# Another written order for a fused attention and two-layer kernel: new places for its steps, twelve element sums on another engine, longer early fillers, input buffers named by group

## The chip, the cores and the metric

The kernel runs on one core of one Trainium2 chip. The metric is the device time of one launch in microseconds (us). Before the change three runs took 276.94, 276.41 and 276.31 us; the median, 276.41 us, is the time before. The profile is of one further execution, told of below.

Five engines with a queue each work side by side: PE (TensorE, the matrix products), DVE (VectorE), ACT (ScalarE), POOL (GpSimd) and SP (SyncE, here a queue that only issues DMAs). Each takes its own instructions strictly in the order in which the program emits them; between engines only semaphores order the work.

## The reference

```
scores = (q_c @ k_c.T) / sqrt(64)          # per batch and head, chunks of 64 rows
scores = scores - max(scores)
attn   = exp(scores); attn = attn / (sum(attn) + 1e-9)
x      = attn @ v_c                        # 4608 tokens x 512
h      = x @ w_in                          # 512 -> 2048
g      = max(0.01 * h, h)
out    = g @ w_out                         # 2048 -> 512, float32
```

q, k and v are float32 of shape (8, 8, 576, 64): 8 batches, 8 heads, 576 rows. Attention is only inside chunks of 64 rows.

## The kernel before

**Groups.** The 4608 tokens are 36 groups of 128 tokens (`u` = 0 to 35). POOL issues the DMAs that bring q and k of a group from HBM and cast them to fp16 (`load_q`, `load_k`, line 93; steps `arrive`), those of v (`load_v`, `load_v_rows`) and the weights. For groups 0 to 9 PE turns q and k (`stage_tq`, `stage_tk`, steps `pe_t`); from group 10 on SP issues DMA transposes (`stage_t`, steps `t`), POOL copies the turned q into its zero-padded place (`stage_q2`, steps `p`, line 446). Then for each group: scores on PE (`s`, line 453), row maximum, subtraction (`m`, `b` on DVE), exponential (`x` on ACT), sum, addition of 1e-9 and reciprocal (`z` on DVE: three instructions, lines 479, 481 and 483), division (`n`, line 489, on DVE or POOL), a second turning (`e` on PE, or `d`: a DMA transpose that SP issues), the product with v (`v` on PE, line 519) and the copy into the ring `xT` (`a` on ACT, line 532).

**Blocks.** The two layers work on blocks of tokens: four of 128 and eight of 512 (`BLOCKS`). Blocks 0 to 5 do the first layer plainly (`mm1`, line 187), blocks 0 to 3 the second as well (`mm2`, line 212). All else uses a fast scheme that makes seven products out of eight: in the first layer steps `f j h i m` (block, half, slice, product m = 1 to 7; line 325), in the second layer steps `m2 j.m.p` (block, product, half; line 373). It needs sums of its operands: of the weights once (`wf`, `vf`), of x for each block (`xf j.h.0` to `.3`, lines 281 and 285) and of g for each block (`sf j.0` to `.3`, in `g_form`): `sf 0` = a21 + a22, `sf 1` = `sf 0` - a11, `sf 2` = a11 - a21 in place (line 350), `sf 3` = a12 - `sf 1` in place (line 352). An `sf` has 128 x 2048 elements of fp16. `sf 0` feeds product 5, `sf 1` product 6, `sf 2` product 7 and `sf 3` product 3. ACT and DVE take the products out of PSUM: copies (`d`, `u2`, `u3`), sums (`+u2`, `+u3`, `+d`, line 237) and the leaky function (`gu2`, `gu3`, `g11`, `g21`, line 198). Two 512-token halves of g (`gT`) and three output buffers (`osb`) turn over; SP issues the saves.

**Order.** A planner has searched an order beforehand; the kernel holds the result. The planning code builds a list of 1403 steps; `ORDER` lists them by number, with the PSUM bank for each step that opens one, and `run()` emits them one by one. What is emitted for one engine therefore keeps the order of that list, and nothing else of the plan (no due time, no duration) reaches the chip. `ON` says for some steps which engine does them. Some entries of `ORDER` hold a filler: `idle()` (line 538) emits useless matmuls on PE ahead of the step, in units of 128 columns, four units to a matmul.

## Time and profile before

| what | us |
|---|---|
| runs: median (lowest, highest) | 276.41 (276.31, 276.94) |
| profiled execution, first to last instruction (its span) | 275.7 |
| what lies around the span, taken as median less span | 0.7 |
| DVE busy | 209.4 |
| ACT busy | 196.3 |
| weight loads busy, beside the matmuls | 230.8 |

How to read it: the span runs from the first to the last instruction of the profiled execution. The profile gives no time of its own for what lies around the span; the 0.7 us is the difference to the median of the runs. A busy PE counts from the start of a matmul to a modelled end, so that two matmuls in a row overlap in the records; the step from start to start is the finer measure.

### The profile page before, as it was taken

To read this page: it belongs to the slowest core of one execution; us is meant where nothing else is said; L and a number is where in the kernel's file an instruction comes from. 1 tells how busy PE (TensorE), PEld (TensorE's weight loads), DVE (VectorE), ACT (ScalarE), POOL (GpSimd) and SP (SyncE) were. 2 spreads that over 40 slices of the span, in tenths; PEclk is the share of its full clock that TensorE was granted. 3 is DMA by queue.
4 is the path that set the end of the run, shared out by engine and by line. 5 is a ranking of instruction groups with operands and counts; after the bars stand their busy time and mean duration, and the time that the engine had idled before them with its cause. 6 is when DMAs were issued, how large, how long until landed. Compare 5 with 4: busy or idle time off the path is not lost.

```text
span 275.7 us, 7655 instructions
## 1 busy us (share of the span) xinstructions
PE 263.9 (96%) x3099; PEld 230.8 (84%) x3099; DVE 209.4 (76%) x376; ACT 196.3 (71%) x370; POOL 158.2 (57%) x199
## 2 busy tenths in 40 slices
PE   4899999999999999999799999999999999999994
PEld 2459678788898899999799999999999989888884
DVE  5786276878889898799778997889998873825462
ACT  6478964767844834899698558899787897467821
POOL 8989685595999991928927888626752020000000
PEclk9999999999999999999999999999999999999999
DMA  9999999999999999999999999969972051040016
GB/s 133 158 190 179 179 167 175 134 157 168 172 160 148 173 173 183 132 138 223 129 131 198 138 173 199 153 148 131 212 154 40 0 137 58 0 155 0 30 49 231
DMA packets 163635, 38.64 MB, mean 140 GB/s; under 512 B 154640, under 2 KB 159248, under 8 KB 163600
## 3 DMA queue, kind: packets, MB, share of 16 engines
q0 software_dynamic: 114384, 18.09, 101.9%
q1 hardware_dynamic: 48176, 19.80, 40.1%
q8 instruction: 24, 0.39, 0.6%
q10 hardware_dynamic: 1040, 0.26, 0.4%
q14 instruction: 11, 0.09, 0.1%
HBM read 36.70 MB, written 9.44 MB: 167 GB/s over the span
## 4 chain that ended last, share of the span: by engine, by line
PE 87%; DMA 5%; ACT 5%; POOL 1%; issue 1%; POOLq 0%
PE oA L373 20%; PE hA L325 14%; PE hT L187 13%; PE oC L373 10%; PE hC L325 7%; PE oB L373 5%; PE oP L212 5%; PE hB L325 4%; PE Sp L453 3%; DMA KT<-k_in 3%; PE xp L519 3%; DMA k_in<-in_k_dram 2%; PE idle L538 1%; ACT VB L118 1%; ACT xT L532 1%; ACT gT L198 1%
## 5 line engine op out<-in xcount | busy, mean ns | idle before, releaser
L373 PEld LDWEIGHTS <-gT 128*128 128x128 f16 x640 | 61.3, 98 | 6.7
L489 POOL TENSOR_TENSOR en<-ex,zi 128x512 f16<-128x512 f16 x23 | 26.5, 1153 | 48.4 <-DVE zi L483 17.3
L237 DVE TENSOR_TENSOR tmp<-hC,tmp 128x512 f32<-128x512 f32 x48 | 32.1, 683 | 20.0 <-PE hC L325 18.3
L187 PE MATMUL hT<-xT,w_inT 128*128 128x128 f16 (+1 forms) x512 | 46.0, 246 | 1.0 <-ACT xT L532 0.9
L187 PEld LDWEIGHTS <-w_inT 128*128 128x128 f16 x512 | 39.4, 98 | 4.7 <-issue 1.3
L325 PEld LDWEIGHTS <-VF 128*128 128x128 f16 x512 | 39.4, 98 | 2.7
L93 POOL DMA_DIRECT2D q_in<-in_q_dram x39 | 33.6, 866 | 5.2 <-DMA w_outT<-in_moe_w_out_dram 2.1
L93 POOL DMA_DIRECT2D k_in<-in_k_dram x39 | 33.6, 865 | 2.3 <-DMA k_in<-in_k_dram 1.2
L446 POOL COPY QZ<-QT 64x512 f16<-64x512 f16 x52 | 33.2, 639 | 2.7 <-DMA QT<-q_in 0.5
L201 ACT ACTIVATE tmp<-hA 128x512 f32<-128x512 f32 x48 | 27.7, 598 | 8.6 <-PE hA L325 8.0
L198 ACT ACTIVATE gT<-hT 128x512 f16<-128x512 f32 x48 | 26.7, 601 | 8.6 <-PE hT L187 8.6
L373 PE MATMUL oA<-WF,gT 128*128 128x256 f16 x256 | 32.5, 273 | 0.0
L325 PEld LDWEIGHTS <-w_inT 128*128 128x128 f16 x384 | 30.2, 98 | 2.3
L463 DVE TENSOR_REDUCE mx<-Sp 128x8 f32<-128x512 f32 x36 | 24.5, 682 | 8.6 <-PE Sp L453 8.5
L198 ACT ACTIVATE gT<-tmp 128x512 f16<-128x512 f32 x48 | 29.6, 629 | 1.2 <-DVE tmp L237 1.2
L473 ACT ACTIVATE ex<-sh 128x512 f16<-128x512 f32 x36 | 22.7, 629 | 10.3 <-DVE sh L467 10.1
L479 DVE TENSOR_REDUCE z<-ex 128x8 f32<-128x512 f16 x36 | 24.3, 676 | 6.2 <-ACT ex L473 6.1
L325 PE MATMUL hA<-XF,VF 128*128 128x128 f16 (+1 forms) x256 | 27.5, 246 | 0.0
L532 ACT ACTIVATE xT<-xp 128x512 f16<-128x512 f32 x36 | 21.2, 599 | 8.7 <-PE xp L519 8.6
L373 PEld LDWEIGHTS <-S 128*128 128x128 f16 x256 | 24.5, 98 | 2.7
L467 DVE TENSOR_TENSOR sh<-Sp,mx 128x512 f32<-128x512 f32 x36 | 24.4, 683 | 0.5
L201 ACT ACTIVATE hB<-hA 128x512 f32<-128x512 f32 x24 | 13.9, 586 | 12.2 <-PE hA L325 12.1
(77 smaller groups left out, 490.3 us busy)
## 6 DMA issues: line engine op xcount, KB each, us to landing
out_dram<-osb SPq DMA_DIRECT2D x14, 512.0 KB, 4.3
VB<-in_v_dram POOLq DMA_DIRECT2D x14, 288.0 KB, 7.8
q_in<-in_q_dram POOLq DMA_DIRECT2D x31, 128.0 KB, 7.4
k_in<-in_k_dram POOLq DMA_DIRECT2D x31, 128.0 KB, 7.2
w_inT<-in_moe_w_in_dram POOLq DMA_DIRECT2D x8, 256.0 KB, 7.6
w_outT<-in_moe_w_out_dram POOLq DMA_DIRECT2D x4, 512.0 KB, 9.4
out_dram<-osb SPq DMA_DIRECT2D x6, 256.0 KB, 4.9
v_t<-in_v_dram POOLq DMA_DIRECT2D x4, 128.0 KB, 7.6
```

Source lines behind the costliest of these rows:

```text
L93: nc.gpsimd.dma_start(out=t[a - u * G:z - u * G], in_=src[b, :, r:r + z - a, :].rearrange("h p d -> p h d"))
L187: nc.tensor.matmul(out=hT[:, i, :], lhsT=w_inT[:, t, fc * 128:(fc + 1) * 128], rhs=xT[:, t, r0 % RING:r0 % RING + tb], start=(i == 0 and t ...
L198: nc.scalar.activation(out=to, in_=of, func=AFT.Prelu, bias=0.0, scale=1.0, alpha=0.01)
L201: nc.scalar.activation(out=to, in_=of, func=AFT.Copy, bias=0.0, scale=1.0)
L237: (nc.vector if e == "dve" else nc.gpsimd).tensor_tensor(out=to, in0=a, in1=b, op=ALU.add)
L325: nc.tensor.matmul(out=PA[key][:, c, :], lhsT=w[:, t, fc * 128:(fc + 1) * 128], rhs=x[:, t, :], start=(m in (1, 5) and c == 0 and t == 0), ...
L373: nc.tensor.matmul(out=to, lhsT=lhs[:, fc, p * 128:(p + 1) * 128], rhs=rhs[:, fc, :], start=(fresh and fc == 0), stop=(fc == HB - 1), skip ...
L446: nc.gpsimd.tensor_copy(out=QZ[u % NQZ][part, :, :, s, :], in_=QT[u][part].rearrange("p i (e t) -> p i e t", e=2))
L463: nc.vector.tensor_reduce(out=MX[u], in_=SP[u], axis=AXL.X, op=ALU.max)
L467: nc.vector.tensor_tensor(out=SH[u], in0=SP.pop(u), in1=MX.pop(u).unsqueeze(2).to_broadcast((128, 8, CH)), op=ALU.subtract)
L479: nc.vector.tensor_reduce(out=z, in_=E[u], axis=AXL.X, op=ALU.add)
L489: eng.tensor_tensor(out=E[u], in0=ex, in1=ZI.pop(u).unsqueeze(2).to_broadcast((128, 8, CH)), op=ALU.mult)
```

## The change

The code that plans and emits keeps its steps and their numbers; the lists `ORDER` and `ON` are new.

Engines. Of all steps, fourteen are given to another engine. DVE to POOL: `sf 8.2`, `sf 8.3`, `sf 9.3`, `sf 10.2`, `sf 10.3`, `sf 11.3`, and `xf 6.0.3`, `xf 9.0.3`, `xf 10.0.0`, `xf 11.0.3`. POOL to DVE: the divisions `n` of the groups 30, 31, 33 and 34. To allow it, `g_form` and `x_form` take the engine as an argument:

```diff
-        if i == 0:
-            plus(SF[j, 0], a21, a22)
+        if i == 0:
+            plus(SF[j, 0], a21, a22, e)
...
-            (nc.gpsimd if j >= POOL_S else nc.vector).tensor_tensor(out=a21, in0=a11, in1=a21, op=ALU.subtract)
-        else:
-            (nc.gpsimd if j >= POOL_S else nc.vector).tensor_tensor(out=a12, in0=a12, in1=SF[j, 1], op=ALU.subtract)
+            minus(a21, a11, a21, e)
+        else:
+            minus(a12, a12, SF[j, 1], e)
```

(`POOL_S` and `POOL_X` were 20, more than any block, so these sums all ran on DVE before.)

Order. On each engine most steps stand a few places elsewhere: 358 of PE's 447 steps (2.7 places on average, 23 at most), 274 of ACT's 368, 214 of DVE's. The stretch around the second-layer sums of block 8 and the end, by engine, read from `ORDER`:

```
block 8, DVE before : +u2 8.0.3, xf 9.0.0, b 30, xf 9.0.2, xf 9.0.1, sf 8.0, xf 9.0.3, sf 8.1, z 30, sf 8.2
block 8, DVE after  : m 30, xf 9.0.1, +u2 8.0.3, b 30, xf 9.0.2, sf 8.0, m 31, b 31, sf 8.1, +u2 of 7, +u3 9.0.0, +u3 9.0.1,
                      z 30, z 31, n 30, +u2 9.0.1, m 32, +u2 9.0.0, n 31
block 8, POOL after : n 29, xf 9.0.3, arrive 35 (q), sf 8.2, p 33.1, arrive 35 (k), v_in 7, p 33.0, sf 8.3
end, PE before      : f 11.0.3.4, f 11.0.3.3, m2 10.4.0, 11.1.1, 10.4.1, 11.2.0, 11.2.1, 11.5.0, 11.5.1, 11.6.0, 11.6.1,
                      11.7.0, 11.7.1, 11.4.0, 11.3.0, 11.3.1, 11.4.1
end, PE after       : f 11.0.2.3, f 11.0.3.4, m2 11.1.1, 10.4.0, 10.3.0, 11.2.0, 10.3.1, 11.2.1, 11.5.0, 11.6.0, 11.6.1,
                      11.7.0, 11.5.1, 11.7.1, 10.4.1, 11.3.0, 11.4.0, 11.3.1, 11.4.1
end, ACT after      : d 11.0, d 11.1, gu2 11.0.2, gu2 11.0.3, u2 11.0, ...
end, DVE before     : +u2 11.0.3, +u2 of 10, sf 11.0, sf 11.1, sf 11.2, sf 11.3
end, DVE after      : +u2 11.0.2, +u2 11.0.3, sf 11.0, sf 11.1, +u2 of 10, sf 11.2
end, POOL after     : sf 9.3, xf 11.0.3, sf 10.2, sf 10.3, sf 11.3 (before: POOL has nothing there)
```

On SP the transposes keep nearly their order; `t 22` (k) goes from behind the save of block 5 to ahead of the last save of block 4. On POOL `make_identity` goes from the sixth to the first place, and the early loads are in another order: before q1, k1, k2, w_in (2 parts), identity, q2, q3, three of v, k3; after identity, q1, k1, k2, one part of w_in, q2, one part of w_in, q3, k3, one part of w_in, three of v.

Fillers. Before there are seven, of 21, 3, 47, 13, 9, 9 and 6 units (108); after nine, of 39, 28, 12, 14, 32, 5, 25, 30 and 11 units (196), all ahead of or at the first `mm1`. The nine stand close together: nearly every step of PE up to there has one ahead of it.

Buffers. Tiles that took the next free buffer of a tag now take one by the number of their group:

```diff
-    def k_tile():
-        return sbp.tile([128, H, D], FP16, name="k_in", tag="k_in", bufs=NIN)
+    def in_tile(what, u):
+        return sbp.tile([128, H, D], FP16, name=what, tag=f"{what}{u % NIN}", bufs=1)
...
-    def osb_tile():
-        return sbp.tile([128, 2, d_model], FP32, name="osb", tag="osb", bufs=3)
+    def osb_tile(n):
+        return sbp.tile([128, 2, d_model], FP32, name="osb", tag=f"osb{n % 3}", bufs=1)
```

and so for `gT`, `KT`, `QT`, `et`, `en`, `ex`, `sh`, `mx`, `z`. The q buffers were four of two groups each and are eight of one group each. Code for loading q in pairs, which nothing called, is gone. The new dependences in the planning lists (`after`) change nothing that is emitted.

## The prediction

> **What bounds the kernel now.** First the page: busy shares and slices. Then the waits of PE, then PE's own places of waiting in the timeline.

> ```profile
> PE 263.9 (96%) x3099; PEld 230.8 (84%) x3099; DVE 209.4 (76%) x376; ACT 196.3 (71%) x370; POOL 158.2 (57%) x199
> PE   4899999999999999999799999999999999999994
> POOL 8989685595999991928927888626752020000000
> ...
> PE kp L411 <- POOL ident masks.py:199: 2.1, 1, 2.1
> PE Sp L453 <- DMA KT<-k_in: 1.7, 1, 1.7
> PE idle L538 <- DVE zeros L157: 1.5, 1, 1.5
> PE kp L411 <- DMA k_in<-in_k_dram: 1.1, 1, 1.1
> PE hT L187 <- ACT xT L532: 0.9, 2, 0.7
> PE Sp L453 <- ACT QZ L118: 0.4, 1, 0.4
> ```

> PE bounds it: busy 96%, all slices full but the first two, one in the middle and the last. The required matmuls are the same after the change, so only three things can move the end: when PE's steady work starts, how long it waits inside, how long the tail is. Inside there are two kinds of waits to win: 1.7 us for a turned k (group 22, at 134.7 us) and 0.9 us, in two places, for xT.

> ```profile
> 152.62 3.49 PE oA L373 x32
> ...
> 255.02 1.04 PE L373 MATMUL oC<-w_outT,gT 128*128 128x256 f16 x8
> ```

> In the chain 32 matmuls of 256 columns take 3.49 us: 0.109 each, 0.87 for an `m2` step of eight, 0.44 for an `f` step of four. The timeline's record of eight lasts 1.04, 0.17 more: ends are modelled, so each wait is about 0.17 longer than its row says.

> **The change part by part.** *Waits that go.* `s 22` stands two `m2` steps (1.74 us of PE work) later in the new order and the transpose of k 22 two places earlier in SP's queue; that covers 1.7 + 0.17. After `v 9` and `v 11`, PE now has 0.87 and 0.6 us more to do before the first `mm1` of the two halves of block 5, which covers 0.9 in two places. Three waits: 1.7 + 0.9 + 3 x 0.17 = **-3.1 us**. If the landing of other transposes takes their place, up to all of this comes back.

> *The front.* PE's first `mm1` starts at 19.98.

> ```profile
> 7.60 0.53 PE L538 MATMUL idle<-XF 128*128 128x384 f16 x1
> 9.92 0.61 PE L411 MATMUL kp<-ident,k_in 128*128 128x128 f16 x4 [1.05 <-DMA k_in<-in_k_dram]
> ...
> 10.76 4.16 PE L538 MATMUL idle<-XF 128*128 128x512 f16 x12
> ...
> 15.64 0.87 PE L538 MATMUL idle<-XF 128*128 128x512 f16 x4
> 16.87 0.41 PE L453 MATMUL Sp<-KT,QZ 128*128 128x64 f16 x8 [0.36 <-ACT QZ L118]
> 17.11 0.65 PE L538 MATMUL idle<-XF 128*128 128x512 f16 x3
> ...
> 18.04 0.65 PE L538 MATMUL idle<-XF 128*128 128x512 f16 x3
> ...
> 19.20 0.49 PE L538 MATMUL idle<-XF 128*128 128x512 f16 x2
> ...
> 19.98 2.17 PE L187 MATMUL hT<-xT,w_inT 128*128 128x128 f16 x32
> ...
> 16.84 2.44 ACT L118 ACTIVATE VB<-v_t 64x256 f16<-64x256 f16 x6
> ```

> The new first filler (39 units) fits where PE runs 2.4 us of filler and waits 2.1. The other fillers now take 0.53 + 4.16 + 0.87 + 0.65 + 0.65 + 0.49 = 7.35 us for 87 units; nine late units take 0.65 less 0.17, 0.054 each. The 157 new ones are 8.5 us at that, +1.1, against waits of 1.05 and 0.36 that they fill: -0.3. On the other side `a 0`, which the first `mm1` needs, stands behind six VB copies on ACT (16.84 to 19.28), and the v loads now come behind a k load and a part of w_in more. POOL's queue is past the identity (about 0.6 us) one after the other; a k load issues in 0.87, so v comes 1 to 2 us later, while ACT, held up until 15.62 by the late turning of q, is free earlier. I take **0**, between -0.7 and +0.8.

> *Sums on POOL.* DVE had time for them under PE's work; the question is what a long POOL instruction does to DVE. The form groups and three places of the timeline:

> ```profile
> L350 DVE TENSOR_TENSOR gT<-gT 128x2048 f16<-128x2048 f16 x8 | 9.6, 1206 | 0.0
> L446 POOL COPY QZ<-QT 64x512 f16<-64x512 f16 x52 | 33.2, 639 | 2.7 <-DMA QT<-q_in 0.5
> L489 POOL TENSOR_TENSOR en<-ex,zi 128x512 f16<-128x512 f16 x23 | 26.5, 1153 | 48.4 <-DVE zi L483 17.3
> ...
> 87.54 1.04 POOL L489 TENSOR_TENSOR en<-ex,zi 128x512 f16<-128x512 f16 x1
> 87.76 0.84 DVE L481 TENSOR_SCALAR ze<-z 128x8 f32<-128x8 f32 x1
> ...
> 116.63 1.06 POOL L489 TENSOR_TENSOR en<-ex,zi 128x512 f16<-128x512 f16 x1
> 116.84 1.01 DVE L285 TENSOR_TENSOR XF<-xT 128x256 f16<-128x256 f16 x1
> ...
> 190.45 0.17 DVE L481 TENSOR_SCALAR ze<-z 128x8 f32<-128x8 f32 x1
> 190.65 0.20 DVE L483 RECIPROCAL zi<-ze 128x8 f32<-128x8 f32 x1
> 190.77 1.18 DVE L350 TENSOR_TENSOR gT<-gT 128x2048 f16<-128x2048 f16 x1
> 191.09 1.75 POOL L489 TENSOR_TENSOR en<-ex,zi 128x512 f16<-128x512 f16 x1 [2.51 <-DVE zi L483]
> ```

> `ze` lasts 0.17, but 0.84 when a division runs on POOL, and ends with it. The x sum lasts 1.01 and ends 0.16 after POOL's division. The other way round, the division takes 1.75 instead of 1.04 when DVE's sum was there first. So of a POOL instruction and a DVE instruction with two SBUF inputs (or `ze`), the second waits for the whole of the first. Before, POOL's longest was 1.04 for 512 elements. An `sf` has 2048: 4 x 1.04 = 4.16 us, taken; not under 4 x 0.64 = 2.6 (the copy with one input), not over 4.6 (the mean of 1.153).

> [...]

> *Block 8.* Let E be the end of `f 8.0.3.3`, the last product that `sf 8.0` needs. DVE does `+u2`, `b 30`, `xf 9.0.2` (0.68, 0.68, 0.41; ACT's leaky step lies beside), so `sf 8.0` runs from about E+2.6 to E+3.8. POOL has had time for `xf 9.0.3` and one DMA issue and starts `sf 8.2` at E+4.0 (it starts 0.24 after its releaser at 191.09). DVE does `m 31` and `b 31`, which read PSUM, and wants `sf 8.1` at E+5.2: it waits until E+8.0 and ends at E+9.2. PE between E and `m2 8.6.0`: two `m2`, twelve `f`, three small steps, 1.74 + 5.2 + 0.7 = 7.7. PE waits 9.3 - 7.7, about **+1.5** (0 with 2.6 us on POOL; 2.0 with 4.6). DVE is then some 2.9 us behind, and POOL, behind two copies and two issues, takes `sf 8.3` about when DVE wants `ze 31` and `n 30`. Those would wait up to 4 us; then `d 30`, `d 31`, and `v 30`, `v 31` on PE are late by 0 to 3 us: **+0.7**, the lower half, as four more us of PE work lie ahead of them.

> *The end.*

> ```profile
> 259.47 1.67 ACT L198 ACTIVATE gT<-tmp 128x512 f16<-128x512 f32 x3
> ...
> 261.17 1.23 DVE L237 TENSOR_TENSOR S<-gT 128x2048 f16<-128x2048 f16 x1 [0.73 <-ACT gT L198]
> ...
> 262.44 1.23 DVE L234 TENSOR_TENSOR S<-S,gT 128x2048 f16<-128x2048 f16 x1
> ...
> 263.58 1.22 DVE L350 TENSOR_TENSOR gT<-gT 128x2048 f16<-128x2048 f16 x1
> 264.71 1.22 DVE L352 TENSOR_TENSOR gT<-gT,S 128x2048 f16<-128x2048 f16 x1
> ...
> 267.95 0.38 ACT L201 ACTIVATE tmp<-oA 128x256 f32<-128x256 f32 x1
> ```

> Now the four sums run in a row on DVE ahead of their products. After: let F be the end of `f 11.0.2.3`. `m2 11.1.1` ends at F+1.31, ACT's `d 11.1` (0.38) at F+1.85, two leaky steps (0.56) at F+3.0; `sf 11.0`, `sf 11.1` end at F+5.5; `+u2` of block 10 ends at F+6.2, and only then comes `sf 11.2`. POOL's `sf 11.3` needs `sf 11.1` and `m2 11.2.1`, which ends at F+0.44+6 x 0.87 = F+5.7: it starts at F+6.0, ahead of `sf 11.2` by 0.2, and holds it until F+10.0; `sf 11.2` ends at F+11.2. PE reaches `m2 11.7.0` three steps after `m2 11.2.1`, at F+8.3. It waits **+3.0** (1.4 at 2.6 us, 3.4 at 4.6; 0.1 if DVE is first, since `sf 11.3` then ends when `m2 11.3.0`, four steps further, comes due). The tail behind the last matmul keeps its steps.

> *The rest.* `sf 9.3` behind `n 35` has about 4.3 us until `m2 9.3.0`, `xf 11.0.3` may come between `sf 10.0` and `sf 10.1`: +0.3 (0 to 1.4). The divisions on DVE cost 0.7 where PE does not wait. Buffers by number: 0, the same distance of reuse; `osb` of block 11 waits for the save of 10.0, some 2 us ahead of need.

> **Sum** against the profiled execution: 275.7 - 3.1 + 0 + 1.5 + 0.7 + 3.0 + 0.3 = 278.1 us of span; with the 0.7 between span and median, **278.8 us**.

> **The rivals.**
> *The sums are hidden* (the other side): DVE is first at both places, or POOL's sum is near 2.6 us, and only the waits go: 275.7 - 3.1 + 0.3 + 0.7 = 273.6. For it: at the end the lead is 0.2 us, in which each of ACT's and POOL's starts counts; the slice row has POOL empty there. It decides from `sf 11.2` starting before F+6.0. Against it: three rows of full waiting, and in block 8 a lead of 1.2 us.
> *One lock only*: the end alone, 275.7 - 3.1 + 3.0 + 0.3 + 0.7 = 276.6; block 8 alone, 275.8.
> *Block 8 runs away*: `ze 31` and `n 30` wait the whole 4 us, +3 instead of +0.7, or a wait for another turned tile stays: 281.

> **How the numbers follow.** Forecast 0.43, hidden 0.27, one lock 0.20, runaway 0.10. About 0.2%, 0.55 us, is what a measurement can tell from no change: same is 275.86 to 276.96. Faster: the hidden case and a fifth of the one-lock case, 0.31. Same: the rest of it, 0.16. Slower: 0.53. The forecast's own range is 277.3 to 280.3 (POOL's sum at 2.6 or 4.6 us). The whole range reaches to the centre of the hidden case and to the runaway: 273.4 to 281.0. Both signs hold much of it.

> **What would show it.** POOL rows of 128x2048 near 4.2 us; a DVE sum `sf 8.1` and `sf 11.2` of 4 to 5 us instead of 1.2, with PE's `oA` (L373) waiting for DVE 1.5 and 3.0 us. No wait of `Sp` for KT near 135, none of `hT` for xT in block 5. First `mm1` between 19.3 and 20.8. I am wrong if the DVE sums keep 1.2 us beside POOL's.

## The result and the profile after

The changed kernel takes 301.47 us (median of four runs, 298.93 to 302.83) where the kernel before took 276.36 in the same session: 1.0906 of it, interval 1.0843 to 1.0970, so 25 us slower. The forecast was 278.8 with 281.0 as its upper end: slower, but by a tenth of this. Ratios leave disturbed executions out (one of `old_lists` took 1554.57 us, the profiled one of `new_order_short` 347.74), so where a median with its range and a ratio differ below, the ratio is the number to read.

The page of the changed kernel, busy shares and slices:

```profile
PE 274.3 (92%) x3120; PEld 233.5 (78%) x3120; DVE 225.6 (76%) x370; ACT 196.0 (66%) x370; POOL 186.7 (63%) x205
...
PE   7999999999999999998899999858999999499964
...
POOL 9989765767978997494798691997060241550310
PEclk9999999999999999999999999997999999889978
```

The slices of PE that were full now have three holes, at slices 26 to 28, 35 and 39 (7.5 us each: some 187 to 209, 254 to 261 and 284 to 291 us), and in or behind each of them the granted clock of PE (PEclk, the share of full speed that PE is allowed) drops, to 0.50 for 3.41 us each time, which it never did before (1.00 in every stretch of that execution). The waits of PE name the holes (us in total, times, longest):

```profile
PE oA L355 <- DVE S L216: 4.1, 1, 4.1
PE hA L307 <- DVE osb L219: 3.5, 1, 3.5
PE oA L355 <- DVE gT L216: 2.7, 1, 2.7
PE xp L491 <- DMA et<-en: 1.7, 2, 1.0
PE hA L307 <- ACT hB L183: 1.5, 1, 1.5
...
PE Sp L425 <- POOL QZ L418: 1.2, 2, 1.0
PE hA L307 <- DVE XF L216: 0.7, 1, 0.7
```

The lines are those of the changed kernel. Line 216 is `minus`, the subtraction of an `sf` or `xf`; line 219 is `plus`, here the sum that writes an output buffer. Of the rest, 307 is a first-layer and 355 a second-layer product, 425 the scores, 491 the product with v, 461 the division, 453 `ze` (the addition of 1e-9), 418 the copy of a turned q, 183 a copy on ACT. The timeline of the changed kernel at these places, DVE, POOL and PE together (start, duration, engine):

```profile
191.28 2.67 DVE L216 TENSOR_TENSOR XF<-xT 128x512 f16<-128x512 f16 x1
191.50 1.06 POOL L461 TENSOR_TENSOR en<-ex,zi 128x512 f16<-128x512 f16 x1
192.51 1.15 POOL L216 TENSOR_TENSOR XF<-xT,XF 128x512 f16<-128x512 f16 x1
...
195.18 4.05 POOL L216 TENSOR_TENSOR gT<-gT 128x2048 f16<-128x2048 f16 x1 [0.64 <-DVE S L219]
196.33 3.98 DVE L216 TENSOR_TENSOR S<-S,gT 128x2048 f16<-128x2048 f16 x1
200.24 0.68 DVE L219 TENSOR_TENSOR osb<-oC,tmp 128x512 f32<-128x512 f32 x1
200.97 0.60 PE L307 MATMUL hA<-xT,w_inT 128*128 128x256 f16 x4 [3.47 <-DVE osb L219]
203.43 4.05 POOL L216 TENSOR_TENSOR gT<-gT,S 128x2048 f16<-128x2048 f16 x1
203.73 3.78 DVE L453 TENSOR_SCALAR ze<-z 128x8 f32<-128x8 f32 x1
209.73 0.60 PE L307 MATMUL hA<-XF,VF 128*128 128x256 f16 x4 [1.48 <-ACT hB L183]
...
253.48 4.05 POOL L216 TENSOR_TENSOR gT<-gT 128x2048 f16<-128x2048 f16 x1 [1.16 <-DVE S L219]
253.50 5.11 DVE L216 TENSOR_TENSOR S<-S,gT 128x2048 f16<-128x2048 f16 x1
258.67 2.86 PE L355 MATMUL oA<-WF,S 128*128 128x256 f16 x16 [4.09 <-DVE S L216]
...
280.73 4.05 POOL L216 TENSOR_TENSOR gT<-gT,S 128x2048 f16<-128x2048 f16 x1 [13.45 <-PE oB L355]
280.89 4.97 DVE L216 TENSOR_TENSOR gT<-gT 128x2048 f16<-128x2048 f16 x1
285.92 1.11 PE L355 MATMUL oA<-WF,gT 128*128 128x256 f16 x8 [2.71 <-DVE gT L216]
```

Read it in pairs. A POOL sum lasts 4.05 us, and a DVE sum of 1.2 us or a `ze` of 0.17 us that starts behind it ends only after it: `sf 8.1` takes 3.98, `ze 31` 3.78, `sf 10.1` 5.11, `sf 11.2` 4.97. Behind each pair PE waits. At 191.28 a DVE sum of 0.41 lasts 2.67, over two POOL instructions in a row: the division, whose record starts 0.22 behind its own, and the POOL sum behind that. `sf 8.1`, `sf 11.2` and this sum wait for no semaphore in the trace. So here, other than said ahead of the prediction, semaphores are not all that orders the work of two engines. This holding of one engine by another is called the lock below.

Where the 22.9 us between the two profiled executions (spans of 298.6 and 275.7) lie can be added up from the single matmuls: the distance from start to start less the step's own (0.109 for 256 columns and so on), summed by stretch from the first `mm1` on. What the lowered clock costs is inside these sums. The medians are 25.1 apart, because these two executions are not the median ones: the changed kernel's took 300.56, and the one of before was some 1.1 us longer than its median. The 0.7 us set down ahead of the prediction as lying around the span is too small by as much; executions of the kernel before with both numbers on record have 1.7 to 1.9 (276.41 with a span of 274.6).

| stretch, us | before | after | difference | forecast |
|---|---|---|---|---|
| first `mm1` | 19.98 | 20.19 | +0.2 | 0 |
| lost from there to 190 | 4.04 | 7.97 | +3.9 | -3.1 |
| 190 to 220 (blocks 8, 9) | 0.05 | 7.90 | +7.9 | +2.2 |
| 220 to 262 (block 10) | 0.07 | 5.95 | +5.9 | +0.3 |
| 262 to the last matmul | 0.01 | 4.62 | +4.6 | +3.0 |
| behind the last matmul | 3.65 | 4.01 | +0.4 | 0 |
| sum | | | +22.9 | +2.4 |

### The profile page after: what moved, and what is told of

It is laid out like the page before. It is cut to its first block, busy times and chain, and to the rows that moved or that the text cites. A ratio compares the mean times of both kernels' runs of the same rounds, so it can differ in the third digit from the quotient of the medians.

```text
span 298.6 us, 7701 instructions
## 1 busy us (share of the span) xinstructions
PE 274.3 (92%) x3120; PEld 233.5 (78%) x3120; DVE 225.6 (76%) x370; ACT 196.0 (66%) x370; POOL 186.7 (63%) x205
## 4 chain that ended last, share of the span: by engine, by line
PE 52%; DVE 23%; DMA 9%; POOL 7%; ACT 4%; issue 3%; SPq 1%; POOLq 0%; DVEq 0%; ACTq 0%
PE oA L355 13%; PE hA L307 8%; PE hT L169 7%; PE oC L355 6%; PE oP L194 4%; PE hC L307 4%; DVE S L216 3%; DMA w_inT<-in_moe_w_in_dram 3%; DMA QT<-q_in 3%; PE oB L355 3%; DVE gT L216 3%; DMA k_in<-in_k_dram 2%; DVE z L451 2%; DVE ze L453 2%; PE hB L307 2%
## 5 line engine op out<-in xcount | busy, mean ns | idle before, releaser
L355 PEld LDWEIGHTS <-gT 128*128 128x128 f16 x640 | 61.8, 99 | 10.5 <-DVE gT L216 3.0
L418 POOL COPY QZ<-QT 64x512 f16<-64x512 f16 x52 | 40.2, 776 | 23.8 <-DMA QT<-q_in 22.3
L219 DVE TENSOR_TENSOR tmp<-hC,tmp 128x512 f32<-128x512 f32 x48 | 31.9, 682 | 18.2 <-ACT tmp L183 11.6
L461 POOL TENSOR_TENSOR en<-ex,zi 128x512 f16<-128x512 f16 x19 | 19.9, 1050 | 33.6 <-DVE zi L455 32.6
L355 PE MATMUL oA<-WF,gT 128*128 128x256 f16 x256 | 33.4, 277 | 2.7 <-DVE gT L216 2.7
L180 ACT ACTIVATE gT<-hT 128x512 f16<-128x512 f32 x48 | 26.8, 597 | 11.4 <-PE hT L169 11.2
L355 PEld LDWEIGHTS <-S 128*128 128x128 f16 x256 | 25.4, 102 | 8.4 <-DVE S L216 4.4
L307 PE MATMUL hA<-XF,VF 128*128 128x128 f16 (+1 forms) x256 | 28.1, 247 | 2.2 <-ACT hB L183 1.5
L216 POOL TENSOR_TENSOR gT<-gT,S 128x2048 f16<-128x2048 f16 x4 | 16.2, 4060 | 19.1 <-PE oB L355 19.1
```

The source lines that it names most:

```text
L180: nc.scalar.activation(out=to, in_=of, func=AFT.Prelu, bias=0.0, scale=1.0, alpha=0.01)
L216: (nc.vector if e == "dve" else nc.gpsimd).tensor_tensor(out=to, in0=a, in1=b, op=ALU.subtract)
L219: (nc.vector if e == "dve" else nc.gpsimd).tensor_tensor(out=to, in0=a, in1=b, op=ALU.add)
L307: nc.tensor.matmul(out=PA[key][:, c, :], lhsT=w[:, t, fc * 128:(fc + 1) * 128], rhs=x[:, t, :], start=(m in (1, 5) and c == 0 and t == 0), ...
L355: nc.tensor.matmul(out=to, lhsT=lhs[:, fc, p * 128:(p + 1) * 128], rhs=rhs[:, fc, :], start=(fresh and fc == 0), stop=(fc == HB - 1), skip ...
L418: nc.gpsimd.tensor_copy(out=QZ[u % NQZ][part, :, :, s, :], in_=QT[u][part].rearrange("p i (e t) -> p i e t", e=2))
```

## The experiments

The theory after this reading, **lock**: the ten sums on POOL (six `sf` and four `xf`; the title counts twelve) hold DVE, PE waits for DVE, and the clock drops behind the wait. The rivals: the **written order** itself costs the time, or the **buffers** named by number add waits.

**The sums back on DVE** (`sums_dve`):

```diff
+    ON.update({('sf', 8, 2): 'dve', ('sf', 8, 3): 'dve', ('sf', 9, 3): 'dve', ('sf', 10, 2): 'dve', ('sf', 10, 3): 'dve', ('sf', 11, 3): 'dve',
+               ('xf', 6, 0, 3): 'dve', ('xf', 9, 0, 3): 'dve', ('xf', 10, 0, 0): 'dve', ('xf', 11, 0, 3): 'dve'})
```

> All ten sums that went to POOL (six sf, four xf) are back on DVE; order, fillers, divisions and buffers stay as after the change. Theory 'lock': the waits of PE that follow a DVE instruction held up by a POOL sum go, by the profile of the changed kernel 0.90 + 3.63 + 1.64 + 4.25 + 2.87 = 13.3 us, and with them what the lowered clock costs behind the three longest, about 1.6 each, 4.9: 301.5 - 18.2 = 283, between 281 and 286; granted clock 1.00 again; PE still waits some 5 us in all between 130 and 190 us. Rival 'written order': the order itself is what costs, and the time stays above 295.

Measured 287.71 (286.93 to 288.52), ratio 1.0412 (1.0352 to 1.0473): 13.8 us of the 25 go. The lock is the larger part, but 18.2 were expected, and some 11.4 us over the kernel before stay (4.12%). **Only the buffers** (`old_lists`; the lists `ORDER` and `ON` of before in the changed code):

```diff
-        (5, 0), (59, 0), (60, 0), (0, 0), (55, 0), (62, 0), (1, 0), (64, 0), (57, 0), (63, 0), (2, 0), (65, 0), (4, 0), (66, 0), (52, 0), (58, 0), (54, 0),
+        (55, 0), (0, 0), (56, 0), (62, 0), (1, 0), (59, 0), (60, 0), (64, 0), (61, 0), (2, 0), (57, 0), (63, 0), (65, 0), (3, 0), (66, 0), (4, 0), (52, 0), (5, 0),
...
```

> The changed code with the order, the fillers and the engines of before: only the buffers by group number are left of the change. Theories 'lock' and 'written order' both: the same as before, 276.4 within 0.5. Rival 'buffers': the new names make an instruction wait for a buffer, and the time is over 277.5, up to the whole 25 us.

Ratio 1.0008 (0.9977 to 1.0038): in the order of before the buffers cost nothing that these runs can tell, at most 1 us. In the new order they were not tried by themselves.

**Who asks first at the end** (`end_dve_first`; steps are moved by number, each pair puts the first directly behind the second, here `sf 11.2` behind `sf 11.1`):

```diff
+    for i, j in [(1367, 1366)]:
+        x = next(y for y in ORDER if y[0] == i)
+        ORDER.remove(x)
+        ORDER.insert([y[0] for y in ORDER].index(j) + 1, x)
```

> One DVE step moved: sf 11.2 directly behind sf 11.1, ahead of the last sum of block 10's products. DVE then asks 0.4 us ahead of POOL's sf 11.3 instead of 0.16 behind it. Theory 'lock, the first has it': sf 11.2 lasts 1.2 instead of 5.0, PE does not wait ahead of the product 7 of block 11 (2.87 less) and its clock is not lowered there (1.6 less): 301.5 - 4.5 = 297. Rival 'a sum on POOL costs this wherever DVE stands': no change, 301.5.

Measured 297.07 (295.65 to 298.24), ratio 1.0744 (1.0663 to 1.0825), 4.4 under the changed kernel. The timeline of this kernel at the end:

```profile
281.59 1.22 DVE L216 TENSOR_TENSOR gT<-gT 128x2048 f16<-128x2048 f16 x1
...
282.03 4.70 POOL L216 TENSOR_TENSOR gT<-gT,S 128x2048 f16<-128x2048 f16 x1 [13.46 <-PE oB L355]
```

Same instructions, same engines; now POOL's sum is the second, waits for DVE (4.70 for 4.05), and PE, which needs it last of all, waits for nothing. In both orders the sum whose record starts first keeps its length (4.05 on POOL, 1.22 on DVE) and the other is held; the starts are 0.16 and 0.44 us apart.

**The clock** (`end_fill`; 13 matmuls of filler ahead of product 7 of block 11, in the place of the wait):

```diff
-(1383, 0)
+(1383, (52, 6))
```

> 52 units of filler (13 matmuls, 2.8 us) ahead of product 7 of block 11, in the place where PE waits 2.87 us. Theory 'the clock is lowered because PE stood idle': the granted clock stays full to the end, the matmuls behind the wait follow each other at 0.109 us, and the time falls by 0.7 to 1.6 us, with the wait itself still there. Rival 'the slow matmuls come from something else, such as the port or the operands': the 0.7 to 1.6 us stay.

Ratio 1.0840 (1.0757 to 1.0924) against 1.0906 (1.0843 to 1.0970) for the changed kernel: the intervals overlap, so the time alone decides nothing. The profiles do: from the end of product 6 to the end of the last matmul the changed kernel takes 11.54 us (283.05 to 294.59), this one 9.87 (282.36 to 292.23), with the filler covering the wait: 1.67 less. The same step, product 5 of the second half, first row of the changed kernel, then of this one:

```profile
286.83 1.91 PE L355 MATMUL oC<-WF,S 128*128 128x256 f16 x8
```

```profile
286.11 1.04 PE L355 MATMUL oC<-WF,S 128*128 128x256 f16 x8
```

Operands and engines are the same, so the 1.91 for 1.04 comes from the idle time ahead of it.

**The order by itself** (`engines_old`: as `sums_dve`, and the four divisions on POOL again):

```diff
+    ON.update({('sf', 8, 2): 'dve', ('sf', 8, 3): 'dve', ('sf', 9, 3): 'dve',
...
+               ('n', 30): 'pool', ('n', 31): 'pool', ('n', 33): 'pool', ('n', 34): 'pool'})
```

> The ten sums on DVE and the four divisions on POOL again: all engines as before the change; of the change only the order, the fillers and the buffer names are left, and the buffer names cost nothing (old_lists). The run sums_dve took 287.7, so some 11 us are not the sums. Theory 'order': the divisions matter little, 286 to 289. Rival 'divisions': four more instructions of 0.68 us on DVE make it late where it frees PSUM banks for PE, and the time falls to 283 or less.

Measured 286.45 (285.65 to 288.31), ratio 1.0387 (1.0353 to 1.0421). The divisions matter little (about 1 us, inside the intervals). The order with its fillers costs 10.5 us, the moved engines some 15 on top of it, of which 13.8 went with the ten sums. By stretch `engines_old` loses 6.70 up to 190 us (4.04 before), 3.57 from 190 to 220 (0.05) and 0.3 after; its first `mm1` is at 22.05 in this execution, at 19.96 in `sums_dve2`. The fillers all stand ahead of the first `mm1`, so what they cost by themselves, which no run separates, is in the front. **Once more for the profile** (`sums_dve2`, the kernel of `sums_dve`):

> sums_dve once more, for its profile: the profiled execution there had a granted clock of 0.949 from end to end, though its time is that of its other executions, which had 0.993 or more. Expected: clock 0.99 or more and waits of PE of 12 to 15 us in all after the first mm1, several small ones between 20 and 215 us on turned tiles and on banks that DVE frees, and none over 1 us after 215. Rival: a wait over 2 us behind 215, which would be a second mechanism in the tail.

It took 286.85, with 13.2 us lost in all and no long wait behind 215, as expected. **The sums alone, in the old order** (`old_pool6`):

```diff
+    ON.update({('sf', 8, 2): 'pool', ('sf', 8, 3): 'pool', ('sf', 9, 3): 'pool', ('sf', 10, 2): 'pool', ('sf', 10, 3): 'pool', ('sf', 11, 3): 'pool'})
```

> The order, fillers and buffers of before, with the six sums sf 8.2, 8.3, 9.3, 10.2, 10.3 and 11.3 on POOL and nothing else. Theory 'lock': each POOL sum holds DVE for about 4 us where DVE asks at the same moment or later, and the time rises by 5 to 18: 281 to 294. Rival 'only the new order meets the lock': within 1.5 of 276.4, since DVE's sums stand elsewhere.

Measured 279.10 (279.00 to 280.47), ratio 1.0123 (1.0096 to 1.0149): 3 us, less than the theory (5 to 18) and more than the rival (within 1.5). The timeline of this kernel:

```profile
237.03 4.17 POOL L216 TENSOR_TENSOR gT<-gT 128x2048 f16<-128x2048 f16 x1 [11.50 <-DVE S L219]
238.41 3.88 DVE L216 TENSOR_TENSOR S<-S,gT 128x2048 f16<-128x2048 f16 x1
242.35 1.92 PE L355 MATMUL oA<-WF,S 128*128 128x256 f16 x16 [1.05 <-DVE S L216]
...
265.12 1.22 DVE L216 TENSOR_TENSOR gT<-gT 128x2048 f16<-128x2048 f16 x1
265.37 4.88 POOL L216 TENSOR_TENSOR gT<-gT,S 128x2048 f16<-128x2048 f16 x1 [18.83 <-DVE S L216]
```

The lock is met here too (in block 10 a DVE sum lasts 3.88), but there PE has more other work ahead of the product and waits 1.05 instead of 4.09, and at the end DVE asks first. The price of a POOL sum is set by what stands beside it in the order.

**What the order costs by.** One place first (`u2_first`: `engines_old` with `+u2` of block 7 directly behind `sf 8.0`):

```diff
+    for i, j in [(895, 1028)]:
...
```

> engines_old (286.45) with one DVE step moved: the sum +u2 of block 7, whose products were done 2 places of PE's first-layer work before, stands directly behind sf 8.0 instead of behind the maximum and the subtraction of group 31 and sf 8.1. It frees the PSUM bank that the product 1 of slice 2 of block 9 opens; there PE waits 2.41 us. Theory 'the new order frees this bank too late': the wait goes, 286.45 - 2.4 = 284.0; sf 8.1 is 0.6 later, which PE does not see. Rival 'DVE is behind here with all its work': the wait comes back at the next product that DVE has to serve, and the time stays within 1 of 286.45.

Measured 285.23 (284.50 to 287.15), ratio 1.0345 (1.0291 to 1.0400): 1.2 under `engines_old`, between the two forecasts, and the intervals overlap. The waits of PE in `engines_old`, and then in `u2_first`:

```profile
PE hA L307 <- DVE osb L219: 2.2, 1, 2.2
```

```profile
PE xp L491 <- DMA et<-en: 1.5, 1, 1.5
...
PE Sp L425 <- POOL QZ L418: 1.2, 3, 0.7
```

The wait went, and these grew from 0.5 and 0.4: the matmul records of `u2_first` lose 10.95 us in all, those of `engines_old` 10.56. Then **the order cut in two** (`new_compute`: new on PE, ACT and DVE, old on POOL and SP; `new_queues`: the reverse). Both are `old_lists` with one list, merged from the old and the new one; its first line in `new_compute` and in `new_queues`:

```diff
+        (59, 0), (0, 0), (60, 0), (55, 0), (1, 0), (62, 0), (64, 0), (57, 0), (63, 0), (2, 0), (65, 0), (66, 0), (3, 0), (52, 0), (4, 0), (54, 0), (53, 0),
...
+        (55, 0), (5, 0), (56, 0), (62, 0), (0, 0), (59, 0), (60, 0), (1, 0), (64, 0), (61, 0), (57, 0), (2, 0), (63, 0), (65, 0), (4, 0), (66, 0), (58, 0),
...
```

> The new order and fillers on PE, ACT and DVE, with the order of before on POOL and SP (loads, turnings, copies, divisions, saves); only p 32 stands two POOL steps earlier, because s 32 does. All engines as before the change. engines_old, with all five orders new, took 286.45, 10.5 over before. Theory 'the compute engines' order': with little slack ahead of the steps that free PSUM banks and feed turned tiles, the loss stays: 284 to 290. Rival 'the queues' order' (later landings of turned tiles, loads in another order): it goes, 276.4 to 279.

> The other half: the order and fillers of before on PE, ACT and DVE, the new order on POOL and SP, engines as before the change; only the last transpose of k stands one place earlier. Theory 'the compute engines' order': 276.4 to 279. Rival 'the queues' order': 284 to 290. If both halves cost 5 or more, what counts is how the two fit each other, and the trace should show more DVE time lost behind POOL's copies and divisions in both (7.3 us before, 16.5 in engines_old).

Measured 301.04 (296.63 to 301.70) and 293.41 (290.18 to 295.04, ratio 1.0572, 1.0471 to 1.0673). Each half costs more than both together (286.45), so neither forecast time was met, and the cut cannot say to which half the 10.5 us belong: the mixture brings costs of its own, new waits between the halves. DVE waits in `new_compute` once for a save of the old order:

```profile
DVE osb L219 <- DMA out_dram<-osb: 6.1, 1, 6.1
```

More DVE time is lost behind POOL in both, as the second expectation named for this case: summing, over all DVE instructions beside a POOL instruction, what they last beyond the quick ones of their form gives some 7 us before, 17 in `engines_old`, 13 in each half, and 30 in the changed kernel (which ones count as quick moves these by about 1 us). **Is that the cause?** (`new_order_short` and `new_order_short2`: `engines_old` with short copies, which leave out 56 of 64 columns of each turned q; `old_order_short`: `old_lists` with the same.)

```diff
-        nc.gpsimd.tensor_copy(out=QZ[u % NQZ][part, :, :, s, :], in_=QT[u][part].rearrange("p i (e t) -> p i e t", e=2))
+        nc.gpsimd.tensor_copy(out=QZ[u % NQZ][part, :, :, s, :8], in_=QT[u][part].rearrange("p i (e t) -> p i e t", e=2)[:, :, :, :8])
```

> engines_old (286.45) with POOL's copies of the turned q cut to 8 of 64 columns (52 copies from group 10 on; the scores of those groups are therefore not those of the reference). All steps, waits and orders stay, but a copy holds DVE's sums, and is held by them, for some 0.1 us instead of 0.64 to 0.79. Theory 'collisions of POOL's copies and DVE's sums cost the new order its time': the 9.2 us that DVE loses behind copies go, and most of the 10 us with them: 278 to 282. Rival 'the new order waits for other things': 284 to 286.5.

> The same cut (8 of 64 columns in the 52 copies) in old_lists, the order of before: the yardstick for new_order_short. DVE loses 4.7 us behind copies there, but PE waits only some 3 us in all: both theories 275 to 276.7. If new_order_short comes within 4 us of this run, the collisions with copies are most of what the new order costs; if it stays 9 or more above it, they are not.

> new_order_short once more (copies of the turned q cut to 8 of 64 columns in the new order), because its profiled execution was disturbed and says nothing of the waits. Its undisturbed times stood 2.1% over the kernel before, old_order_short 0.55% under it. Expected again 281 to 284. The waits of PE that are left after the first mm1 tell the rest: theory 'lock' wants them behind DVE instructions held up by POOL's divisions; rival 'slack' wants them on DMA landings and on DVE steps that were not held up, as in the half-and-half runs.

Ratios 1.0212 (1.0161 to 1.0262) and 1.0368 (1.0326 to 1.0410) for the same kernel twice, 0.9945 (0.9915 to 0.9976) for the old order. In `new_order_short2` DVE loses some 7 us behind POOL, as little as before the change, and the kernel still takes 282.70 to 286.86. The two sessions differ by more than their intervals: the short copies save 4.8 us of the 286.45 in the one and 0.5 in the other, and 1.5 in the old order, so 7.4 or 11.7 us stay between the two orders. These collisions are then a smaller part of the 10 us, by these runs between nothing and 5; a closer figure is not shown. What PE waits for in `new_order_short2`:

```profile
PE xp L491 <- DMA et<-en: 3.5, 4, 1.6
```

Turned tiles. Of each group that SP turns for the second time, take the time from the landing of `et` to the start of its product `v` on PE: before, the median of 25 groups is 4.6 us and no group has less than 1; in `engines_old` it is 2.4, and 5 groups have less than 1; in `new_order_short2` 2.3 and 7. For the turned k the new order has more room (7.8 instead of 4.9 us): it moved room from the one to the other. But this room does not go with the time. In `old_order_short`, at 275.19, 5 groups have less than 1 (median about 4), and in `new_compute`, at 301.04, it is one group (median about 4). That the lost room costs the 10 us is therefore not shown.

**Short waits of the kernel before** (`s22_early`, in the kernel before; `before_tuned` with three moves more):

```diff
+    for i, j in [(776, 529), (777, 671)]:
...
+    for i, j in [(776, 529), (777, 671), (556, 357), (396, 326), (398, 327)]:
...
```

> The kernel before with two steps moved: the transpose of k 22 ahead of the last save of block 5 in SP's queue, and the scores of group 22 two first-layer steps (0.87 us) later on PE. Theory 'the wait for KT of group 22 is all that this place costs': its 1.7 us go, 276.4 - 1.7 = 274.7. Rival 'the landing is set by the load of the DMA engines': the transpose lands when it landed before and the next turned tiles land later: 275.8 to 276.5.

> s22_early with the two waits for xT in block 5 shortened as well: the attention products of groups 9 and 11 each go ahead of one second-layer step on PE (0.87 us), and ACT copies the turned group 9 ahead of a copy of block 4. Theory 'each wait is worth its length': 0.4 for the first, 0.38 for the second beside the 1.7 of group 22: 276.4 - 2.5 = 273.9, and 0.5 to 1 below s22_early. Rival 'the run-to-run spread of the landings takes it': no difference to s22_early, 275.4.

275.43 (274.11 to 276.92), ratio 0.9980 (0.9958 to 1.0002), and 275.29, ratio 0.9965 (0.9939 to 0.9992). In `s22_early` PE no longer waits for a turned k, and of the 1.7 us of that wait some 0.5 come out in the time, which the interval does not tell from nothing. `before_tuned` is faster than both kernels, by a third of a per cent (1.0 us), where 2.5 us were expected: in its profile PE has a new wait, ahead of `v 27`.

```profile
PE xp L519 <- DMA et<-en: 0.9, 1, 0.9
```

## Why the prediction was wrong

Its mechanism, the lock, was found where it looked, and it looked at too few places; and the term for the waits that go counted only the waits of the old profile.

- *The end* held. Forecast +3.0 from a lead of POOL of 0.2 us; measured lead 0.16, wait 2.87 (start to start). The sum on POOL, taken at 4.16, lasts 4.05. `end_dve_first` shows that the lead decides there (POOL 0.16 ahead or DVE 0.44), and with DVE first PE does not wait, as its other case (0.1) said.
- *Block 8* had the mechanism right and the place and size wrong. `sf 8.1` ended late as forecast, but PE did not get to `m2 8.6.0`: it stopped earlier, at product 1 of slice 2 of block 9, because `+u2` of block 7, which frees that PSUM bank, stands behind `sf 8.1` on DVE. The term counted who needs the sum, not who needs what is queued behind it. The second lock, `ze 31` behind `sf 8.3`, was given 0.7; PE waited 1.64 for it, not by way of `d 30` and `v 30`, but because the sums behind `ze 31` on DVE came late and ACT's copy (209.10) waited for them. `xf 9.0.2` behind a division and `xf 9.0.3` cost another 0.90. In the stretch 190 to 220 the sums cost 7.90 - 3.57 = 4.3 over `engines_old`, against 2.2.
- *The rest*, put at +0.3 (0 to 1.4) for `sf 9.3` and `xf 11.0.3`, did not look at `sf 10.2` at all; block 10 cost 5.9. `sf 10.0` releases both `sf 10.2` on POOL and `sf 10.1` on DVE; their starts are 0.02 us apart and POOL has the lock. PE waits 4.25, start to start.
- *The clock* was no term of the sum. In the changed kernel three waits were followed by 3.41 us at half clock, which cost 1.6 to 1.7 us each; for the last of them `end_fill` shows it.
- *Waits that go*, -3.1, came out as +3.9 and is the term furthest off. The wait of `s 22` did go. But the working followed only the three old waits to their new places, and took each at its full length; in the old order all three are worth 1.0 us (`before_tuned`). What the new places of all other steps cost was put at nothing. `engines_old` shows that this cost is mostly the order's (6.70 of the 7.97 lost up to 190), and the short copies that the lock with copies is the smaller part of its 10 us. How the rest divides between room ahead of `v`, banks freed late by DVE, the front and the fit of the queues stays open.
- *Buffers* and *tail* held: 0 and +0.4. *Front* held between these two executions, +0.2, but by luck in part: in the six profiled executions with the old order the first `mm1` starts at 18.63 to 19.98 us, and the 19.98 is the kernel before; in eight with the whole new order (`new_order_short` left out) at 19.90 to 22.05. By the medians, 19.2 and 20.1, the new front costs some 0.9, above the 0.8 that the range allowed.
- The *range* does not follow from the terms. With POOL's sum at 2.6 us they give 278.8 - 1.5 - 1.6 = 275.7, at 4.6 us 278.8 + 0.5 + 0.4 = 279.7, where 277.3 to 280.3 is written. The measured time is far outside of either.
- The rival "block 8 runs away" was the right kind of case, but its price, 281, took one lock at a time. Four locks, each with a drop of the clock or a queue behind it, add.

The size: some 15 us for the moved engines with their clock, nearly all of it the ten sums, and some 10 for the order.

## What to carry to other kernels

Before a long instruction goes to POOL, list for each place which DVE instruction of the kinds that were held here (a sum of 1.2 us lasted up to 5.11, a `ze` of 0.17 lasted 3.78) comes due during it and what is queued behind that one; in block 10 a start 0.02 us earlier went with a wait of 4 us, and at the end, where DVE was put first, the wait went. A reordering that removes the visible waits is not worth their sum: removing them gave 1.0 us of 2.5, and the other steps, of which a profile without waits does not say how near to waiting they are, can take far more. No one figure tried here, neither the room ahead of `v` nor DVE's time lost behind POOL, foretold the time of a new order; measure it. And a wait of PE cost more than its length where the granted clock fell to 0.50 behind it: a filler in the wait of 2.87 us took that part, 1.67 us, away.

## What the runs showed of the hardware

```profile
198.03:201.45 3.42, 0.48 (x6) 1.00 0.00 0
201.45:204.86 3.41, 3.41 (x25) 0.50 1.23 197
204.86:208.27 3.41, 3.39 (x31) 1.00 1.30 86
```

In two executions the length of the wait alone did not decide: the same wait of 2.25 us (2.41 from start to start) falls mostly into one slot in `sums_dve2` and into two in `engines_old`. (`engines_old` has no fall there; its slots are counted, as an estimate, from the start, where four turning products last 0.56 us at 6.23 and 0.39 at 6.63; 6.60 is 56 slots ahead of 197.75.) The former:

```profile
196.16:199.57 3.41, 1.16 (x18) 1.00 1.18 76
199.57:202.98 3.41, 3.41 (x19) 0.50 1.43 213
```

The latter, where the clock stays:

```profile
197.75:201.16 3.41, 1.58 (x21) 1.00 0.32 89
201.16:204.58 3.42, 3.42 (x34) 1.00 0.27 87
```

Ahead of the three falls in the changed kernel PE was busy for 0.48, 0.80 and 0.86 us of a slot of 3.41 (the slots from 198.03, 256.06 and 283.37), ahead of the one in `sums_dve2` for 1.16. With 1.58 in `engines_old`, 1.90 in the kernel before (133.19 to 136.61) and 1.93 in the changed kernel (252.65 to 256.06) the clock stayed. Where between 1.16 and 1.58 of 3.41 us the limit lies, these traces do not show.

**A clock of 0.949 that cost nothing, in one execution.** The profiled one of `sums_dve` had this clock throughout:

```profile
core 0: 286.1 us, clock 0.949
```

Its stretches have 0.94 to 0.96, and it took 287.85 us where the other executions, at 0.993 and more, took 286.93 to 288.52. Why the lower clock cost no time is not shown. **POOL's copies last longer as well**: the form group of the copies in `engines_old` has 790 ns each, where the kernel before had 639:

```profile
L418 POOL COPY QZ<-QT 64x512 f16<-64x512 f16 x52 | 40.9, 790 | 20.7 <-DMA QT<-q_in 12.9 <-PE hC L307 6.3
```
